# Six buffers of tap weights, due times for their steps, and sums moved from VectorE to GpSimd in a convolution with soft MoE

## The chip, the cores and the metric

The kernel runs on one core of a Trainium2 chip. Its engines are called PE (TensorE; PEld is its loading of weights), DVE (VectorE), ACT (ScalarE), POOL (GpSimd) and SP (SyncE, which issues the DMAs here). The metric is the device time of one execution in microseconds (us).

## The reference

Tokens: B = 8 sequences of S = 3584 with D = 192 channels, in 8 heads of 24. All numbers are float32. Each token brings 7 weights a head, which go through a softmax and then weigh the last 7 tokens; the result x goes through a soft MoE of 8 experts with 4 slots each.

```
w = weight_gen - max(weight_gen, -1);  w = exp(w);  w = w / (sum(w, -1) + 1e-9)
x[b,s,h,:] = sum over k of w[b,s,h,k] * x_pad[b, s+k, h, :]      # 6 zeros in front
logits = x @ phi                                                 # 28672 x 32
d = exp(logits - logits.max(0));  d /= d.sum(0) + 1e-9           # over the tokens
slot_in = d.T @ x;  per expert: slot_out = relu(slot_in @ w1[e]) @ w2[e]
c = exp(logits - logits.max(1));  c /= c.sum(1) + 1e-9           # over the slots
out = c @ slot_out
```

## The kernel before

**Convolution.** A group is 104 tokens of one sequence, 4 blocks of 26. On PE a block and head quartet is one matmul of a 128x26 band against 100 columns of x: the band holds the 7 weights of each token on its diagonals, so that 32 rows of x (for each of 4 heads) give 26 tokens. Seven groups are a *step* s (40 steps), two groups are a *pair* (140 pairs), eight pairs are a *unit* (16 units of 8 pairs and two of 6). So a step is 3.5 pairs. The sum of a token's weights comes out of the same matmul, from a column of ones in x, and the division is done behind it.

**The chain of taps of one step.** The raw weights ("taps") of a step are loaded by SP (`loadw`, 196 KB, L178); DVE takes the maximum of each seven (`tap_top`, L185); POOL subtracts it in place (`tap_sub`, L190); ACT takes the exponential and puts it into `places` (`tap_exp`, L199, two instructions); DVE transposes 32 x 32 blocks into `byrow` (`tap_turn`, L203); and POOL multiplies that by a mask into the band, in two halves of two instructions each (`band_make`, L214, columns 0 to 14 and 14 to 28; an operation of 588 elements a partition and one of 140). There are NTAP = 4 buffers of taps, two of the maxima, NPL = 2 of `places` and `byrow`, NBAND = 3 bands. x is loaded in half steps by four DMAs each (`loadx`, L175) into NXH = 5 buffers.

**The rest of the loop.** Behind `conv` (L238) of a pair: ACT copies the sums of weights (`ws`, L248), DVE takes their reciprocal (L254) and multiplies (L259, into `tm`), PE transposes (L273, `pt`), ACT copies that out (L278, `cm`). Once per unit PE makes the logits (L302), DVE the columns' maximum (L309, L311 `mq`), PE turns it (L325), ACT the exponential, DVE a transpose (L347, `dt`), and PE the dispatch (L366, `acb`). The logits are saved in `LT`, in 16 halves of sequences of 18 or 17 groups.

**Order.** The order of DVE, ACT, POOL and PE is the order in which the program emits their instructions; SP's queue is in order, and its DMAs are issued one after the other, each after the waits of its own buffer. The opening (L377 to L431) is written by hand. The loop comes from a planner: `op(engine, cost, reads, writes, f, ...)` adds an operation with an estimated cost, `late` is time that its result needs beyond the engine's, and `due` is how long behind its readiness it is to begin at the latest. `model` (L622) computes from these the latest start of each and lays them out engine by engine, the one with the earliest latest start first; its order of starts is the order of emission (L688). The times in it are estimates of the planner.

**Behind the loop** the experts are computed, and then comes the *stores' part*: for each of 49 pieces of the output PE multiplies c with the slots' outputs (`rows`, L821), DVE or ACT evicts the result from PSUM into `big` (`leave`, L828), and SP stores it (L830). c is made from `LT` by `soft`, in seven steps per half: row maximum (DVE, L78), subtraction (POOL, L80), exponential (ACT, L83), row sum (DVE, L86), + 1e-9 (ACT, L88), reciprocal (DVE, L90), multiplication (POOL, L92). Five halves are done in the loop, some behind it, and eight in the stores' part, one step per part; `turn` (L450, DVE) transposes a finished half for PE.

Of the kernel before, what the change touches and what calls it, by code (L numbers as in the profile page):

```python
# [10 lines left out]
ALU = mybir.AluOpType  # L11
# [30 lines left out]
def conv_soft_moe(ctx, tc, xh, wh, phi, w1a, w1b, w2, out):  # L42
# [30 lines left out]
    def soft(pool, h, step):  # L73
# [10 lines left out]
        elif step == 3:  # L84
            sm = sms[h] = pool.tile([128, 18, 1], F32, tag="sm", name=f"sm{h}", bufs=4)[:, 0:n]
            V.tensor_reduce(out=sm, in_=lt, axis=AX.X, op=ALU.add)  # L86
# [17 lines left out]
    NTM, NCV, NTAP, NPL, NBAND = 2, 4, 4, 2, 3  # L104
# [36 lines left out]
    for t in places:  # L141
        G.memset(t, 0.0)
# [5 lines left out]
    make_identity(nc, ident)  # L148
    near = keep.tile([128, 128], F32, name="near")
# [227 lines left out]
    loadw(0)  # L377
    loadx(0)
    loadw(1)
# [10 lines left out]
    A.copy(xbd[:, 2:4, 1], zero.unsqueeze(1).to_broadcast([128, 2, HBC * GX]))  # L390
    warm(1)
    band_make(0, 0, 8, V)
    tap_top(1)
    G.memset(xbd[:, 2:4, 0], 0.0)
    tap_sub(1, G)
    G.memset(xbd[:, 2:4, 2], 0.0)
    tap_exp(1)
    for h in (0, 1):
        G.memset(xbd[:, 4, h], 0.0)
# [13 lines left out]
    for h in (2, 3):  # L413
        A.copy(xbd[:, 4, h], zero.to_broadcast([128, HBC * GX]))
    band_make(0, 22, HB, V)
    loadx(4)
    for t in tms:
        V.memset(t[:, :, 0:1], 1.0)
        V.memset(t[:, :, 2 * D + 1 : 2 * D + 2], 1.0)
    band_make(1, 6, 14)  # L420
    conv_inv(0)
    conv_out(0)
    conv_out(1)
    band_make(1, 14, HB)
# [5 lines left out]
    for q in range(4):  # L430
        G.memset(qneg[32 * q : 32 * q + 32, q : q + 1], -1.0)  # L431

# [78 lines left out]
    for late, what in ((1.0, x_of(2)), (1.7, x_of(3)), (0.0, ("w", 2)), (1.0, ("w", 3)),  # L511
                       (5.0, x_of(4)), (0.0, ("band", 1, 0)), (2.5, ("band", 1, 1)),
                       (2.5, ("r", 1))):
# [5 lines left out]
    for k in range(1, SLOTS):  # L519
# [32 lines left out]
        for s in made.get(k, ()):  # L552
            op(VE, 0.5, [("w", s % NTAP)], [("top", s % 2)], tap_top, s)
            op(PO, 0.85, [("top", s % 2)], [("w", s % NTAP)], tap_sub, s)
            op(AC, 0.75, [("w", s % NTAP)], [("pl", s % NPL)], tap_exp, s)
            op(VE, 0.6, [("pl", s % NPL)], [("r", s % NPL)], tap_turn, s)
# [382 lines left out]
```

## Time and profile before

| | |
|---|---|
| median of 3 runs | 331.64 us (330.34 to 334.37) |
| the profiled execution | 332.66 us |
| its span in the profile | 330.9 us |
| mean granted TensorE clock | 0.935 |
| busy: PE, PEld, DVE, ACT, POOL | 275.4, 209.1, 248.3, 165.4, 202.6 us |
| DMA | 72.77 MB, mean 220 GB/s |
| first store issued | 268.91 us |

The times in the profile are those of one execution, counted from the span's start. A row of the timeline has start, length, engine, line, operation, output <- input, shape and count, and in brackets the engine's idle time before it with what ended it. A row of the windows has its length, the busy time of PE, PEld, DVE, ACT and POOL with the numbers of instructions, the granted clock (1.00 is full), the DMA share and GB/s.

### The profile page before, as it was taken

The numbers are of one execution on the slowest core, as the hardware profiler recorded it, in microseconds if no ns is written. First come the engines' busy times: TensorE is split into PE (matmuls) and PEld (weight loads), VectorE is DVE, ScalarE is ACT, GpSimd is POOL, SyncE is SP. The second block draws the span as 40 slices with busy tenths as digits, with TensorE's granted clock in tenths as the row PEclk, the third lists the DMA queues.
The fourth block names the chain that finished last, engine by engine and source line by source line (L and its number), as shares of the span: only waits on it lengthen the run. The fifth ranks groups of instructions, "written<-read, shape, count | busy, mean of one in ns | idle before, by whom it ended". The sixth has DMA issues, their size and how long they took to land.

```text
span 330.9 us, 16312 instructions
## 1 busy us (share of the span) xinstructions
PE 275.4 (83%) x6816; PEld 209.1 (63%) x6816; DVE 248.3 (75%) x549; ACT 165.4 (50%) x469; POOL 202.6 (61%) x265
## 2 busy tenths in 40 slices
PE   7779799999999988999799969899978976777500
PEld 6657678787788776888688858788857821212100
DVE  6676688888898987888687688787646689999500
ACT  7466254565645654555365445554441356656300
POOL 8989366977879786787767648487005554740000
PEclk9799799999999999999999999999999995579855
DMA  4565657676766657766776576666892049999995
GB/s 136 152 195 163 183 154 231 187 204 184 218 189 205 187 145 216 205 187 173 210 210 204 166 203 182 202 188 172 306 414 113 4 155 371 365 387 398 402 401 230
DMA packets 33000, 72.77 MB, mean 220 GB/s; under 512 B 7072, under 2 KB 12576, under 8 KB 32928
## 3 DMA queue, kind: packets, MB, share of 16 engines
q1 hardware_dynamic: 32928, 71.74, 67.9%
q8 instruction: 54, 0.88, 1.1%
q14 instruction: 18, 0.15, 0.2%
HBM read 49.35 MB, written 22.36 MB: 217 GB/s over the span
## 4 chain that ended last, share of the span: by engine, by line
PE 55%; DMA 14%; DVE 10%; POOL 7%; issue 5%; ACT 3%; SPq 1%; DVEq 0%; ACTq 0%; POOLq 0%
PE cv L238 25%; PE pt L273 12%; PE acb L366 6%; DMA out<-big 6%; PE ls L302 6%; POOL band L214 4%; DMA big<-xh 4%; DMA taps<-wh 4%; DVE big L828 2%; PE hpb L752 2%; PE so L773 2%; PE po L821 1%; POOL taps L190 1%; DVE sm L86 1%; SPq L175 1%
## 5 line engine op out<-in xcount | busy, mean ns | idle before, releaser
L214 POOL TENSOR_TENSOR band<-byrow,mask 128x588 f32<-128x588 f32 (+3 forms) x158 | 120.7, 795 | 41.9 <-DVE byrow L203 37.8
L238 PE MATMUL cv<-big,band 128*26 128x100 f32 x4480 | 121.2, 253 | 12.8 <-DVE band L214 3.6
L238 PEld LDWEIGHTS cv<-big,band 128*26 128x26 f32 x4480 | 103.1, 128 | 26.1 <-issue 16.7
L259 DVE TENSOR_TENSOR tm<-cv,ws 128x384 f32<-128x384 f32 x140 | 71.8, 551 | 6.2 <-DVE ws L254 0.9
L278 ACT COPY cm<-pt 128x312 f32<-128x312 f32 x140 | 52.1, 424 | 46.8 <-PE pt L273 46.1
L248 ACT ACTIVATE ws<-cv,eps 128x16 f32<-128x16 f32 x140 | 38.1, 273 | 55.9 <-PE cv L238 45.7
L273 PE MATMUL pt<-ident,tm 122*128 122x122 f32 x420 | 59.7, 278 | 1.8 <-ACT cm L278 1.8
L273 PEld LDWEIGHTS pt<-ident,tm 122*128 122x128 f32 x420 | 43.6, 142 | 18.1 <-issue 9.6
L821 PE MATMUL po<-cT,so 32*128 32x468 f32 (+3 forms) x256 | 32.2, 713 | 12.0 <-DVE big L828 11.3
L190 POOL TENSOR_TENSOR taps<-taps,top 128x392 f32<-128x392 f32 x39 | 34.0, 877 | 10.1 <-DVE top L185 5.5
L254 DVE RECIPROCAL ws<-ws 128x32 f32<-128x32 f32 x70 | 23.7, 339 | 20.9 <-ACT ws L248 20.4
L821 PEld LDWEIGHTS po<-cT,so 32*128 32x128 f32 (+1 forms) x256 | 8.8, 185 | 34.9 <-DVE big L828 30.5
L828 ACT COPY big<-po 128x936 f32<-128x936 f32 (+2 forms) x25 | 22.4, 898 | 16.8 <-PE po L821 9.6
L302 PE MATMUL ls<-cm,phi_sb 128*32 128x208 f32 (+1 forms) x576 | 29.2, 334 | 1.4 <-issue 1.3
L185 DVE TENSOR_REDUCE top<-taps 128x56 f32<-128x392 f32 x40 | 21.7, 548 | 11.1 <-DMA taps<-wh 8.1
L366 PE MATMUL acb<-tm,dt 128*32 128x193 f32 x536 | 27.9, 340 | 2.0 <-DVE dt L347 1.5
L828 DVE COPY big<-po 128x884 f32<-128x884 f32 (+2 forms) x24 | 25.4, 1067 | 3.2 <-DMA out<-big 3.0
L199 ACT ACTIVATE places<-taps 128x196 f32<-128x196 f32 x80 | 25.5, 378 | 3.9 <-POOL taps L190 3.7
L203 DVE STREAM_TRANSPOSE byrow<-places 128x448 f32<-128x448 f32 x40 | 25.2, 631 | 2.6 <-ACT places L199 1.5
L92 POOL TENSOR_TENSOR LT<-LT,sm 128x576 f32<-128x576 f32 (+1 forms) x16 | 18.1, 1131 | 12.1 <-DVE sm L90 12.0
L80 POOL TENSOR_TENSOR LT<-LT,rm 128x576 f32<-128x576 f32 (+1 forms) x16 | 18.0, 1131 | 10.7 <-DVE rm L78 10.7
L302 PEld LDWEIGHTS ls<-cm,phi_sb 128*32 128x32 f32 x576 | 18.9, 109 | 6.2 <-issue 2.0
(109 smaller groups left out, 224.4 us busy)
## 6 DMA issues: line engine op xcount, KB each, us to landing
big<-xh SPq DMA_DIRECT2D x320, 87.5 KB, 3.2
out<-big SPq DMA_DIRECT2D x23, 468.0 KB, 6.1
out<-big SPq DMA_DIRECT2D x24, 442.0 KB, 5.8
taps<-wh SPq DMA_DIRECT2D x40, 196.0 KB, 3.3
big<-w SPq DMA_DIRECT2D x8, 768.0 KB, 7.6
w1a_sb<-w1a SPq DMA_DIRECT2D x16, 256.0 KB, 3.1
w1b_sb<-w1b SPq DMA_DIRECT2D x8, 256.0 KB, 3.7
out<-big SPq DMA_DIRECT2D x2, 234.0 KB, 2.4
```

What stands on the lines that cost most here:

```text
L190: eng.tensor_tensor(out=r, in0=r, in1=tops.pop(s).to_broadcast([128, 2 * TJ, KT]), op=ALU.subtract)
L199: A.activation(to, taps[s % NTAP][:, b].rearrange("p (a q) k -> p a q k", q=KT), AF.Exp)
L214: eng.tensor_tensor(out=w[:, j : j + n, l].rearrange("p (a k) l -> p a k l", k=k), in0=r[:, 0:k].unsqueeze(1).to_broadcast([128, n // k, k ...
L238: P.matmul(cv[32 * blk : 32 * blk + T, o : o + 4 * GX], bands[s % NBAND][:, :, bc], xbd[:, j % NXH, :, b * GX : (b + 1) * GX], start=True, ...
L248: A.activation(wss[p // 2][:, p % 2], cvs[p % NCV][:, 0 : 16 * GX].rearrange("p (h w) -> p h w", w=GX)[:, :, GW:], AF.Identity, bias=eps[: ...
L259: V.tensor_tensor(out=tms[u % NTM][:, pr, 1 : 2 * D + 1].rearrange("p (h w) -> p h w", w=GW), in0=cv[:, :, 0:GW], in1=wss[p // 2][:, p % 2 ...
L273: P.transpose(pt[:, i, 0:TR], tm[0:TR, pr, 1 + 128 * i : 129 + 128 * i], ident[0:TR, 0:TR])
L278: copy(cms[u][:, pr].rearrange("p i b j -> p (i b) j"), pts.pop(p).rearrange("p i (b j) -> p (i b) j", j=32)[:, :, 0:T])
L302: P.matmul(lp[32 * blk : 32 * blk + 32, 0:n, par, 0:T], phi_sb[:, 2 * par + i, :], cm[:, 0:n, 1 if i else 2 * par, blk, :], start=(i == 0) ...
L366: P.matmul(ac[32 * q : 32 * q + 32], dt[:, g, :], tm[:, g // 2, o : o + D + 1], start=(g < 4), stop=(g + 4 >= 2 * n))
L821: P.matmul(po[dst : dst + hi - lo, at, 0 : n * T], so[32 * q : 32 * q + 32, lo:hi], cT[32 * q : 32 * q + 32, g0 : g0 + n, 0:T], start=True ...
L828: (V.tensor_copy if done[1] % 2 else A.copy)(ot.rearrange("p (q c) -> p q c", c=n * T), po[:, 0 : len(qs), 0 : n * T])
```

## The change

- NTAP is 6 instead of 4: taps of step s + 5 are loaded where those of s + 3 were.
- In the planner maximum, subtraction, exponential and turn of a step get due times (14, 3, 3 and 4), the bands a lower cost (1.6 instead of 1.8) with `late` 0.5, other costs are adjusted to three digits, and steps up to 2 are left out of it, since the opening has them now.
- The opening is written in another order: taps of step 1 ahead of x, taps of steps 4 and 5 behind `loadx(4)`; maximum, subtraction and exponential of step 1 ahead of the bands of step 0; those of step 2 are in the opening, its subtraction and the second half of the bands of step 1 on DVE; the zeroing of `xbd` (= `big`) is spread in another way over POOL and ACT, and the zeroing of `places` stands behind that of `ident`.
- In the stores' part the row sum is a tree on GpSimd: five additions of 16, 8, 4, 2 and 1 columns of each group's 32, instead of one reduction on DVE. In the loop and behind it the sums stay on DVE.
- Of the first 30 evictions DVE takes two of five instead of every second one (24 of all 49 before, 21 now), ACT the others.

```diff
+    def total(pool, h, to, lt, eng):
+        if eng is V:
+            V.tensor_reduce(out=to, in_=lt, axis=AX.X, op=ALU.add)
+            return
+        n, w = lt.shape[1], NS // 2
+        t = pool.tile([128, 18, w], F32, tag="tree", name=f"tree{h}")[:, 0:n]
+        G.tensor_tensor(out=t, in0=lt[:, :, 0:w], in1=lt[:, :, w:], op=ALU.add)
+        while w > 1:
+            w //= 2
+            G.tensor_tensor(out=t[:, :, 0:w] if w > 1 else to, in0=t[:, :, 0:w],
+                            in1=t[:, :, w : 2 * w], op=ALU.add)
...
-            V.tensor_reduce(out=sm, in_=lt, axis=AX.X, op=ALU.add)
+            total(pool, h, sm, lt, eng)
...
-    NTM, NCV, NTAP, NPL, NBAND = 2, 4, 4, 2, 3
+    NTM, NCV, NTAP, NPL, NBAND = 2, 4, 6, 2, 3
...
     loadw(0)
+    loadw(1)
     loadx(0)
-    loadw(1)
     loadx(1)
     loadw(2)
...
+    tap_top(1)
     tap_turn(0)
-    G.memset(xbd[:, 2:4, 3], 0.0)
+    tap_sub(1, G)
+    tap_exp(1)
     A.copy(xbd[:, 2:4, 1], zero.unsqueeze(1).to_broadcast([128, 2, HBC * GX]))
+    A.copy(xbd[:, 2:4, 3], zero.unsqueeze(1).to_broadcast([128, 2, HBC * GX]))
...
     band_make(0, 0, 8, V)
-    tap_top(1)
...
-    tap_sub(1, G)
...
-    tap_exp(1)
...
     tap_turn(1)
-    loadw(3)
     loadx(2)
     loadx(3)
+    loadw(3)
...
-    band_make(0, 16, 22, V)
+    band_make(0, 16, 24, V)
     band_make(1, 0, 6)
...
+    band_make(0, 24, HB, V)
...
+    band_make(1, 6, 14)
...
+    loadx(4)
+    loadw(4)
+    loadw(5)
...
+    conv_inv(0)
+    conv_out(0)
+    conv_out(1)
+    tap_top(2)
+    tap_sub(2, V)
+    tap_exp(2)
+    band_make(1, 14, HB, V)
...
+            if s > 2:
+                op(VE, 0.53, [("w", s % NTAP)], [("top", s % 2)], tap_top, s, due=14.0)
+                op(PO, 0.88, [("top", s % 2)], [("w", s % NTAP)], tap_sub, s, due=3.0)
+                op(AC, 0.68, [("w", s % NTAP)], [("pl", s % NPL)], tap_exp, s, due=3.0)
+            op(VE, 0.63, [("pl", s % NPL)], [("r", s % NPL)], tap_turn, s, due=4.0)
...
-                op(PO, 1.8, [("r", s % NPL)], [band_of(s, h)], band_make, s, lo, hi)
+                op(PO, 1.6, [("r", s % NPL)], [band_of(s, h)], band_make, s, lo, hi, late=0.5)
...
-        (V.tensor_copy if done[1] % 2 else A.copy)(
+        (V.tensor_copy if done[1] % (5 if done[1] < 30 else 2) in (1, 3) else A.copy)(
...
-                soft(pc, i, part - first)
+                soft(pc, i, part - first, G)
```

In the opening SP's queue stands in another order. Its rows, first of before (taps_84 to taps_87 are the four buffers of taps, big holds x, a row with x4 or x8 is one or two half steps):

```order
L178 DMA taps_84<-wh 128x392
L175 DMA big<-xh 32x700 x4
L178 DMA taps_85<-wh 128x392
L175 DMA big<-xh 32x700 x4
L178 DMA taps_86<-wh 128x392
L178 DMA taps_87<-wh 128x392
L175 DMA big<-xh 32x700 x8
L406 DMA phi_sb<-phi 128x128
L175 DMA big<-xh 32x700 x4
L178 DMA taps_84<-wh 128x392
L175 DMA big<-xh 32x700 x8
```

and then now, with the buffers taps_84 to taps_89:

```order
L190 DMA taps_84<-wh 128x392
L190 DMA taps_85<-wh 128x392
L187 DMA big<-xh 32x700 x8
L190 DMA taps_86<-wh 128x392
L187 DMA big<-xh 32x700 x8
L190 DMA taps_87<-wh 128x392
L416 DMA phi_sb<-phi 128x128
L187 DMA big<-xh 32x700 x4
L190 DMA taps_88<-wh 128x392
L190 DMA taps_89<-wh 128x392
L190 DMA taps_84<-wh 128x392
L187 DMA big<-xh 32x700 x8
```

The taps of step 1 moved ahead of x, those of step 3 behind two half steps of x, and ahead of the sixth half step of x (the last row) there now stand the loads of steps 4, 5 and 6, where there was that of step 4 alone.

In the loop POOL's subtractions stand elsewhere. Before, at the bands of steps 5 and 6 (band_94 is step 5, band_92 step 6; the subtractions of steps 6, 7 and 8 are those of taps_86, taps_87 and taps_84):

```order
L214 TENSOR_TENSOR band_94<-byrow_91,mask_134 128x21x28
L214 TENSOR_TENSOR band_94<-byrow_91,mask_134 128x5x28
L190 TENSOR_TENSOR taps_86<-taps_86,top_558 128x392
L190 TENSOR_TENSOR taps_87<-taps_87,top_657 128x392
L190 TENSOR_TENSOR taps_84<-taps_84,top_792 128x392
L214 TENSOR_TENSOR band_92<-byrow_90,mask_134 128x21x28
L214 TENSOR_TENSOR band_92<-byrow_90,mask_134 128x5x28
```

Now, at the bands of steps 5 and 6 (band_96 and band_94; the subtractions of steps 7 and 8 are those of taps_85 and taps_86):

```order
L202 TENSOR_TENSOR taps_85<-taps_85,top_664 128x392
L226 TENSOR_TENSOR band_96<-byrow_93,mask_136 128x21x28
L226 TENSOR_TENSOR band_96<-byrow_93,mask_136 128x5x28
L226 TENSOR_TENSOR band_94<-byrow_92,mask_136 128x21x28
L226 TENSOR_TENSOR band_94<-byrow_92,mask_136 128x5x28
L202 TENSOR_TENSOR taps_86<-taps_86,top_796 128x392
```

Three subtractions in a row became single ones between halves of bands, each further ahead of its own band.

In the stores' part POOL's queue has the trees. Before, from the subtraction (L80) of one half to multiplications (L92) of others:

```order
L80 TENSOR_TENSOR LT<-LT,rm_5591 128x544
L80 TENSOR_TENSOR LT<-LT,rm_5629 128x576
L92 TENSOR_TENSOR LT<-LT,sm_5604 128x576
L92 TENSOR_TENSOR LT<-LT,sm_5606 128x544
L80 TENSOR_TENSOR LT<-LT,rm_5648 128x544
L92 TENSOR_TENSOR LT<-LT,sm_5626 128x576
L80 TENSOR_TENSOR LT<-LT,rm_5670 128x576
```

Now (L79 and L82 are the tree, L92 is the subtraction and L104 the multiplication):

```order
L92 TENSOR_TENSOR LT<-LT,rm_5593 128x544
L79 TENSOR_TENSOR tree_5639<-LT 128x288
L82 TENSOR_TENSOR tree_5639<-tree_5639 128x18x8
L82 TENSOR_TENSOR tree_5639<-tree_5639 128x18x4
L82 TENSOR_TENSOR tree_5639<-tree_5639 128x18x2
L82 TENSOR_TENSOR sm_5638<-tree_5639 128x18
L79 TENSOR_TENSOR tree_5663<-LT 128x272
```

Between a half's subtraction and its multiplication POOL now also issues its five additions, and the additions of other halves stand there too.

More of the change, by code (lines that the diff above doesn't have):

```diff
@@ L148, in conv_soft_moe @@
     make_identity(nc, ident)
+    for t in places:
+        G.memset(t, 0.0)
     near = keep.tile([128, 128], F32, name="near")
@@ L581, in conv_soft_moe @@
                     op(e, c, lt if step == 0 else [],
-                       [("soft", h), ("rm", h % 2)], soft, pa, h, step, due=8.0 + step)
+                       [("soft", h), ("rm", h % 4)], soft, pa, h, step,
+                       due=8.0 + step)
         if k in dispatched and UNITS[dispatched[k] + 1][1] < UP:
@@ L636, in model @@
                 last[i] = min(last[i], max(begin[j] for j in ops[i][3]) + ops[i][4])
[L637 removed]
+        free = {TE: 0.0, VE: 2.5, AC: 0.3, PO: 1.8, SP: 0.0}
         ends, at = [None] * len(ops), [0.0] * len(ops)
```

38 lines of the change are left out of this document (12 added, 26 removed).

## Prediction

> **What bounds the kernel now.** I began with the waits of the whole span (engine and line, what it waited for, us in total, times, longest) and with the long middle stretch, in which nearly all of the 18 units are convolved.
>
> ```profile
> DVE top L185 <- DMA taps<-wh: 8.1, 6, 2.8
> ...
> POOL band L214 <- DVE byrow L203: 37.8, 23, 4.7
> ```
>
> ```profile
> 32.00:232.00 200.00, 187.72 (x5274) 154.58 (x5262) 161.34 (x379) 106.35 (x346) 146.35 (x184) 0.99 0.68 191
> ```
>
> DVE's maximum waits 8.1 us for taps, in six times, and POOL's bands 37.8 for the turned taps; whether that costs anything, the loop must tell. In the 200 us of the windows row (columns: length, busy time of PE, weight loads, DVE, ACT, POOL, the granted clock, the DMA share, GB/s) PE is busy for 187.72, and no other engine for more than 161.34. PE bounds the loop, and what a change can win there is PE's lost time. To see how much that is I took one PE operation that comes once per unit, the logits of L302, and read its starts in the timeline:
>
> ```profile
> 26.81 0.36 PE L302 MATMUL ls<-cm,phi_sb 128*32 128x208 f32 x4
> ...
> 175.33 0.36 PE L302 MATMUL ls<-cm,phi_sb 128*32 128x208 f32 x4
> ...
> 187.35 0.36 PE L302 MATMUL ls<-cm,phi_sb 128*32 128x208 f32 x4
> ...
> 228.13 0.36 PE L302 MATMUL ls<-cm,phi_sb 128*32 128x208 f32 x4
> ```
>
> The unit from 175.33 to 187.35 has no stall: 12.02 us for 8 pairs, so a step of 3.5 pairs takes about 5.26. From 26.81 to 228.13 there are 15 more such intervals, 201.32 us; at 12.02 they would take 180.3. **21.0 us of the loop are stalls.** The next rows say which of them belong to the chain of taps (load, maximum, subtraction, exponential, turn, band):
>
> ```profile
> 33.80 0.56 DVE L185 TENSOR_REDUCE top<-taps 128x56 f32<-128x392 f32 x1 [2.98 <-POOL band L214]
> ...
> 35.21 0.50 PE L238 MATMUL cv<-big,band 128*26 128x100 f32 x8 [1.79 <-POOL taps L190]
> ...
> 190.32 0.56 DVE L185 TENSOR_REDUCE top<-taps 128x56 f32<-128x392 f32 x1 [2.76 <-DMA taps<-wh]
> ...
> 193.42 0.25 PE L325 MATMUL acb<-mq,sel 128*32 128x5 f32 x8 [2.82 <-DVE mq L311]
> ...
> 208.37 0.56 DVE L185 TENSOR_REDUCE top<-taps 128x56 f32<-128x392 f32 x1 [2.18 <-DMA taps<-wh]
> ...
> 209.86 0.37 PE L366 MATMUL acb<-tm,dt 128*32 128x193 f32 x4 [1.05 <-DVE dt L347]
> ```
>
> ```profile
> DMA to landing us min/median/max: 4.3/4.3/4.3
> ```
>
> ```profile
> 31.95:35.36 3.41, 1.56 (x60) 1.18 (x55) 1.55 (x4) 0.80 (x3) 3.41 (x6) 1.00 0.64 166
> 35.36:38.78 3.42, 3.42 (x45) 2.43 (x41) 2.89 (x7) 0.27 (x1) 0.49 (x1) 0.50 0.67 187
> ```
>
> At 190.32 DVE stands still in front of the maximum L185 for 2.76 us, until the taps land; the small work behind it on DVE (mq, L311) is late, and PE waits 2.82 at 193.42. The same happens at 208.37, where PE loses 1.05. At 33.80 the page names a band as the releaser, but that load was issued at 29.37 and took 4.3 us (the landing row is of this one issue), so it landed at about 33.7: a third wait for taps. PE loses 1.79 at 35.21, and then half its clock: it was busy 1.56 of 3.41 us, and the next 3.42 were granted at 0.50, where about 1.6 us of work is lost. So late taps cost 2.82 + 1.05 + 1.79 + 1.6, with some tenths of slower starts around them (measured start to start), **7.9 us**.
>
> ```profile
> 81.94 0.31 PE L238 MATMUL cv<-big,band 128*26 128x100 f32 x4 [0.50 <-POOL band L214]
> ...
> 124.00 0.52 PE L238 MATMUL cv<-big,band 128*26 128x100 f32 x13 [1.02 <-POOL band L214]
> ...
> 124.13 0.37 SPq L178 DMA_DIRECT2D taps<-wh  x1
> ...
> 129.35 0.40 PE L238 MATMUL cv<-big,band 128*26 128x100 f32 x8 [1.56 <-DMA big<-xh]
> ...
> 158.74 0.32 PE L238 MATMUL cv<-big,band 128*26 128x100 f32 x4 [0.42 <-POOL band L214]
> ```
>
> Three bands came late (0.50 + 1.02 + 0.42, start to start **2.65**). At 124.13 SP had stood before a taps load until the exponential had freed its buffer; the x behind it in that queue came late, and PE lost 1.56 at 129.35 (start to start **1.8**). The remaining 8.7 of the 21.0 are stalls that this change doesn't touch, most of them the "issue" kind.
>
> **The change, part by part.** *Loop.* With six buffers a load is issued two steps earlier, 10.5 us, against a longest wait of 2.8. The 7.9 go, and I see no transfer that comes later for it: the number of bytes and the x loads' places in the queue behind the first steps stay. The due times put maximum, subtraction, exponential and turn ahead: in the new program most turns stand 2 to 6 pairs further before the pair that uses their band (step 8: 8 instead of 4; step 10: 11 instead of 5; step 31: 10.5 instead of 4.5). Each pair is 1.5 us of PE (12.02 / 8). That covers the 2.65 of late bands and, since the exponential is earlier and SP waits for it, the 1.8. Removable: 7.9 + 2.65 + 1.8 = 12.3. What is late next: steps 20 and 22 keep a lead of 4 and 3 pairs (3 and 5 before), and the maxima, now early, stand before work of other chains on DVE; a subtraction that POOL can't take, because its bands wait for free band buffers, leaves ACT in front of the exponential. No row shows these waits; from below they cost 0, from above, at the price of the worst band wait above (1.02) at four places and another half clock (1.6), 5.7, and I take 3.8, nearer to the upper end since leads of 3 pairs are those at which a band was late before. **Loop: −8.5**, between −12.3 and −6.6.
>
> *Opening.* Steps 1 and 2 of the chain go ahead of x and of bands:
>
> ```profile
> 9.88 0.35 PE L238 MATMUL cv<-big,band 128*26 128x100 f32 x5 [1.51 <-DVE band L214]
> ...
> 19.84 1.18 POOL L214 TENSOR_TENSOR band<-byrow,mask 128x588 f32<-128x588 f32 x1 [1.45 <-DVE byrow L203]
> ...
> 20.38 1.59 SPq L175 DMA_DIRECT2D big<-xh  x1
> ...
> 21.45 0.40 PE L238 MATMUL cv<-big,band 128*26 128x100 f32 x8 [1.11 <-POOL band L214]
> ...
> 23.07 0.31 PE L238 MATMUL cv<-big,band 128*26 128x100 f32 x4
> ```
>
> Before, the band of step 2 could start at 19.84, behind its turn. In the new order the chain of step 2 stands before the second band of step 1, and counted with the durations of the trace its turn is done by about 14.8; the pair that waited until 21.45 then can start near 18. The next pair (23.07) needs x that SP issued from 20.38 on; two more taps loads of 196 KB now stand before it in that queue, though its buffer is free sooner, so I put the pair at 20.3: 2.8 earlier. The wait of 1.51 at 9.88 shrinks too, but it lies before the same x. I take −3, between −1 (x as late as now) and −4. Inside it is a loss on DVE, which now takes the subtraction of step 2 and half a band beside POOL's work:
>
> ```profile
> 8.52 1.46 DVE L214 TENSOR_TENSOR band<-byrow,mask 128x252 f32<-128x252 f32 x4
> ...
> 8.69 0.97 POOL L190 TENSOR_TENSOR taps<-taps,top 128x392 f32<-128x392 f32 x1 [0.36 <-DVE top L185]
> ...
> L214 DVE TENSOR_TENSOR band<-byrow,mask x10: 166/306/887, 6.6 to 11.7; 128x252 f32<-128x252 f32 x3, 128x60 f32<-128x60 f32 x3, 128x336 f32<-128x336 f32 x1, 128x80 f32<-128x80 f32 x1
> ```
>
> The longest of DVE's ten bands took 887 ns where the median is 306; it is one of the four that start at 8.52, and POOL subtracted beside it from 8.69 on. So 0.6 us more per meeting, and with two or three meetings about 1.5 us, not all of it before PE. The Trainium skill ("SBUF — State Buffer", section "Who interferes with whom") says that a DVE instruction with two SBUF inputs and a GpSimd one that reads SBUF exclude one another for the whole instruction; the 887 agrees, and taken strictly, with each meeting as long as POOL's 0.87 and 1.18 us, the opening would give −2.5 instead of −3.
>
> *Stores' part.* Here DVE is full and the DMAs are nearly so:
>
> ```profile
> 268.00:304.00 36.00, 25.14 (x196) 6.54 (x190) 35.91 (x54) 23.59 (x36) 17.71 (x16) 0.76 0.92 361
> ...
> 272.00:304.00 32.00, 21.66 (x169) 5.41 (x160) 31.91 (x48) 20.20 (x32) 14.45 (x13) 0.73 0.97 379
> ...
> 300.00:320.00 20.00, 9.13 (x88) 2.40 (x84) 10.56 (x11) 7.56 (x9) 0.00 (x0) 0.80 1.02 401
> ```
>
> ```profile
> L86 DVE TENSOR_REDUCE sm<-LT 128x18 f32<-128x576 f32 x4 | 2.8, 707 | 0.0
> ...
> L828 DVE COPY big<-po 128x936 f32<-128x936 f32 x11 | 12.3, 1117 | 0.6 <-DMA out<-big 0.5
> L828 ACT COPY big<-po 128x936 f32<-128x936 f32 x12 | 11.2, 934 | 4.3 <-DMA out<-big 1.9 <-PE po L821 1.7 <-ACT sm L88 0.5
> ```
>
> ```profile
> L214 POOL TENSOR_TENSOR band<-byrow,mask 128x588 f32<-128x588 f32 x77 | 91.0, 1182 | 41.9 <-DVE byrow L203 37.8 <-PE pt L273 2.4 <-PE cv L238 1.6
> L214 POOL TENSOR_TENSOR band<-byrow,mask 128x140 f32<-128x140 f32 x77 | 32.6, 423 | 0.0
> L92 POOL TENSOR_TENSOR LT<-LT,sm 128x576 f32<-128x576 f32 x8 | 9.3, 1157 | 6.6 <-DVE sm L90 6.5
> ```
>
> ```profile
> 302.33 0.72 DVE L450 STREAM_TRANSPOSE cT<-LT 128x544 f32<-128x544 f32 x1
> ```
>
> ```profile
> out<-big SPq DMA_DIRECT2D x23, 468.0 KB, 6.1
> ```
>
> Undisturbed stores move 401 GB/s, those from 272 to 304 379: 32 × (1 − 379/401) = 1.8 us is all that a freer DVE can win. DVE loses eight sums (8 × 0.7) and three evictions (3 × 1.1), 8.9 of 36 us; ACT gains 3 × 0.93. POOL gains eight trees. From 588 elements at 1182 ns and 140 at 423, one POOL operation costs 186 ns + 1.69 ns per element; the tree of 18 rows writes 288, 144, 72, 36 and 18: 5 × 0.186 + 558 × 0.00169 = 1.9 us, in place of 0.707 on DVE. POOL then has 17.7 + 15 = 32.8 of 36 us. That fits, with 1.5 us to spare before the last turn (302.33). No row shows POOL on pieces of 8, 4 and 2 elements; from below a tree costs one 576-element operation (1.16), from above five of them (5.8). I take the line, which three sizes of row lie on: **−1.2**.
>
> The sum: −3 − 8.5 − 1.2 = −12.7 against the profiled execution's own 332.66 (its span 330.9 and 1.8 around it), so 320.0. That execution lies 1.0 above the median of the runs, so I predict **319** beside 331.64.
>
> **Rivals.** (a) *The new order only moves the stalls.* Every due time is a planner's estimate, and POOL's bands are paced by three buffers whatever stands ahead. For it: the leads of steps 20 and 22. Against: three waits of the loop are a DMA's, which no order restores. Then the loop gives about half, −4.5, and the opening −1.5: 332.66 − 7.2 − 1.0, about 325. (b) *The taps are not the bound.* SP still waits for each exponential at the same place of its queue, and an earlier load could take the DMA share (0.68) that x needs; then x is late where the taps were. Loop −2.65, opening −2, stores 0: 327. (c) *Slower: GpSimd's trees bound the stores.* Pieces of a few elements may cost POOL far more than the line. The last turn starts at 302.3; A store of 468 KB lands 6.1 us after its issue and takes 1.17 at 401 GB/s, so five are queued. POOL has until the last turn, plus two of these five (2.3 us): 302.3 − 268 + 2.3 − 17.7 = 18.9 us for eight trees. From 2.36 us a tree on, 8T − 18.9 is added, and above 3.8 us the kernel is slower than before; at the upper end (5.8) it is +27.5, so 332.66 − 11.5 + 27.5 − 1.0, about 348. The Trainium skill ("GPSIMD Engine Reference", section 4.1 "Engine selection") speaks for this side: it puts free-axis reductions on VectorE and calls two-input elementwise work on GpSimd about twice as slow. By it the tree is a loss of engine time, as in the sum above (1.9 for 0.7), and no row here shows more. (d) *Lock.* DVE and POOL in each other's way take all of the opening's gain: 322.
>
> **How the numbers follow.** Forecast 0.53 (313 to 324), (a) 0.22, (b) 0.10, (c) 0.06, (d) 0.09. The low end is the sum with all bounds good: 332.66 − 1.0 − 12.3 − 4 − 1.8 = 313.6; the high end takes in (a), (b) and (d): 313 to 328. A change below 2%, 6.6 us, is about what a measurement of this kernel can't tell from none: faster means below 325.0, which holds nearly all of the forecast and of (d) and a third of (a): 0.69. (c), in its milder half, and the rest give 0.26 and 0.05.
>
> **What would show it.** Right: no DVE wait for taps over 0.5 us behind the opening; intervals of L302 near 12.3 on average instead of 13.4; the granted clock at 1.0 in the slices at 32 to 40 us; the first L302 near 24; DVE below 30 of the first 36 us of the stores, with 390 GB/s or more. Wrong: PE waits for x where it waited for bands; trees above 2.4 us each; waits of ACT for POOL's subtraction; or the logits' interval unchanged although DVE's waits for the taps are gone. The biggest risk in the sum is the 3.8 for new stalls, which no row measures.

## The result, and the profile after

The changed kernel takes 334.53 us (median) where the kernel before takes 330.68: a ratio of 1.0122 (95% interval 1.0088 to 1.0157), 4 us slower, where 319 was forecast and at most 328 allowed. The opening got faster, by less than forecast; that the loop did isn't shown; the stores' part lost more than was won. Some executions of any of these kernels are a per cent or two longer than the rest: ratios leave them out, medians don't. Stage by stage, from the profiled executions:

| | before | after | forecast |
|---|---|---|---|
| first logits (end of the opening) | 26.81 | 25.88 | −3 |
| 15 intervals of logits (loop) | 201.3 | 198.8 | −8.5 |
| first store issued | 268.91 | 266.69 | |
| first store issued to last store landed | 61.0 | 65.6 | −1.2 |

The loop's 2.5 us lie within what profiles of one loop differ by: the loop of before took 196.6 to 201.3 in its own profile and in those of four runs below that change only the stores (198.8 on the mean), the changed loop 198.8 to 199.7 in three (199.1). The first logits do part: 26.4 to 27.3 in these five profiles, 25.7 to 26.2 in these three.

The timeline's two rows of the logits after, and the windows of the loop and of the first 36 us of the stores (columns as before):

```profile
25.88 0.36 PE L314 MATMUL ls<-cm,phi_sb 128*32 128x208 f32 x4
...
224.67 0.36 PE L314 MATMUL ls<-cm,phi_sb 128*32 128x208 f32 x4
```

```profile
32.00:232.00 200.00, 189.92 (x5309) 156.45 (x5313) 162.52 (x384) 106.69 (x346) 144.52 (x181) 0.99 0.65 192
...
268.00:304.00 36.00, 25.48 (x152) 8.48 (x148) 23.44 (x36) 21.19 (x34) 31.38 (x54) 0.67 0.84 330
```

In the stores DVE is free now (23.44 of 36 us busy instead of 35.91), but the DMAs move 330 GB/s instead of 361: 36 × (361 − 330)/401 = 2.8 us lost there, although the first store of before comes only 0.9 us into this window. The waits of the whole span show that the taps' own waits went as forecast; below them stands PE's wait for x before:

```profile
POOL band L226 <- PE cv L250: 17.9, 13, 3.9
POOL band L226 <- DVE byrow L215: 17.3, 9, 3.9
...
PE cv L250 <- DMA big<-xh: 7.2, 7, 2.2
...
DVE top L197 <- DMA taps<-wh: 2.2, 3, 1.0
```

```profile
PE cv L238 <- DMA big<-xh: 2.1, 3, 1.6
```

DVE waits 2.2 us for taps instead of 8.1, POOL 17.3 for turned taps instead of 37.8. In their place POOL's bands wait 17.9 us for PE to free a band buffer (1.6 before), as rival (a) had said of the three buffers, and PE waits 7.2 us for x (2.1 before).

### The profile page after: what moved, and what is told of

Its sections match the earlier page's. It is cut to its first block, busy times and chain, and to the rows that moved or that the text cites. A ratio compares the mean times of both kernels' runs of the same rounds, so it can differ in the third digit from the quotient of the medians.

```text
span 333.3 us, 16324 instructions
## 1 busy us (share of the span) xinstructions
PE 282.5 (85%) x6816; PEld 214.4 (64%) x6816; DVE 242.8 (73%) x541; ACT 169.3 (51%) x473; POOL 214.9 (64%) x301
## 5 line engine op out<-in xcount | busy, mean ns | idle before, releaser
L226 POOL TENSOR_TENSOR band<-byrow,mask 128x588 f32<-128x588 f32 (+3 forms) x156 | 119.7, 796 | 37.9 <-PE cv L250 17.9
L250 PE MATMUL cv<-big,band 128*26 128x100 f32 x4480 | 122.5, 254 | 15.1 <-DMA big<-xh 7.2
L285 PE MATMUL pt<-ident,tm 122*128 122x122 f32 x420 | 60.5, 281 | 0.7 <-ACT cm L290 0.7
L840 PE MATMUL po<-cT,so 32*128 32x442 f32 (+3 forms) x256 | 37.6, 707 | 11.4 <-ACT big L847 9.9
L202 POOL TENSOR_TENSOR taps<-taps,top 128x392 f32<-128x392 f32 x38 | 33.2, 875 | 13.4 <-ACT ws L260 5.9
L840 PEld LDWEIGHTS po<-cT,so 32*128 32x128 f32 (+1 forms) x256 | 12.5, 189 | 36.0 <-ACT big L847 23.6
L847 ACT COPY big<-po 128x936 f32<-128x936 f32 (+2 forms) x28 | 24.5, 901 | 10.2 <-PE po L840 4.7
L378 PE MATMUL acb<-tm,dt 128*32 128x193 f32 x536 | 26.6, 331 | 0.7 <-DVE dt L359 0.6
L847 DVE COPY big<-po 128x884 f32<-128x884 f32 (+2 forms) x21 | 22.3, 1066 | 5.7 <-PE po L840 3.9
L378 PEld LDWEIGHTS acb<-tm,dt 128*32 128x32 f32 x536 | 17.9, 110 | 4.2 <-DVE dt L359 1.3
L92 POOL TENSOR_TENSOR LT<-LT,rm 128x576 f32<-128x576 f32 (+1 forms) x16 | 18.0, 1132 | 3.7 <-DVE rm L90 3.7
```

The costliest lines, as they stand in the source:

```text
L202: eng.tensor_tensor(out=r, in0=r, in1=tops.pop(s).to_broadcast([128, 2 * TJ, KT]), op=ALU.subtract)
L226: eng.tensor_tensor(out=w[:, j : j + n, l].rearrange("p (a k) l -> p a k l", k=k), in0=r[:, 0:k].unsqueeze(1).to_broadcast([128, n // k, k ...
L250: P.matmul(cv[32 * blk : 32 * blk + T, o : o + 4 * GX], bands[s % NBAND][:, :, bc], xbd[:, j % NXH, :, b * GX : (b + 1) * GX], start=True, ...
L285: P.transpose(pt[:, i, 0:TR], tm[0:TR, pr, 1 + 128 * i : 129 + 128 * i], ident[0:TR, 0:TR])
L378: P.matmul(ac[32 * q : 32 * q + 32], dt[:, g, :], tm[:, g // 2, o : o + D + 1], start=(g < 4), stop=(g + 4 >= 2 * n))
L840: P.matmul(po[dst : dst + hi - lo, at, 0 : n * T], so[32 * q : 32 * q + 32, lo:hi], cT[32 * q : 32 * q + 32, g0 : g0 + n, 0:T], start=True ...
```

## Experiments: the stores' part

Each run is compared with runs of the kernel before on the same chip. Ratios come with 95% intervals; "stores" is first store issued to last landed and "loop" the 15 intervals of logits, both from the run's one profile.

**The parts of the change alone.** The change with the stores' part of before:

```diff
-        (V.tensor_copy if done[1] % (5 if done[1] < 30 else 2) in (1, 3) else A.copy)(
+        (V.tensor_copy if done[1] % 2 else A.copy)(
...
-                soft(pc, i, part - first, G)
+                soft(pc, i, part - first)
```

> The changed kernel with the stores' part of before (sums on DVE, every second eviction on DVE): opening and loop of the change alone. In the two traces the first store comes 2.2 us earlier and the stores take 4.5 us longer. Theory S (the trees cost the 4.5, and opening and loop are a small gain): about 328.5 where before has 330.7, first store near 266.7, from the first store to the end as before, 61 to 61.5 us. Rival R (the stores start 2 us earlier at another place of the throttle's or the DMAs' rhythm and are slow for that): stores' part over 64 us, time as the changed kernel, 334.

Ratio 0.9962 (0.9919 to 1.0005), stores 61.0, loop 199.7, first store at 266.40. The stores are back to their time though they start as early as in the changed kernel: theory S, not R. From 268 to 304 us their DMAs move 381 GB/s, so against stores that start at the same time the trees lose 36 × (381 − 330)/401 = 4.6 us, the whole loss.

The kernel before with `total()` of the change and `soft(..., G)` in the stores, nothing else:

> The kernel before with only the eight sums as trees on GpSimd, evictions as before. Theory S1 (POOL in its order is the stores' bound, and ACT and DVE stand behind its results with the evictions): the stores' part 4 to 5 us longer, 335. Rival S2 (it is the eviction split, more evictions queued on ACT behind ACT's small steps, that costs): no more than +1, 331.7. A gain of 1 would be my forecast's term.

336.05 us, ratio 1.0139 (1.0069 to 1.0209), stores 64.8. The trees alone cost as much as the whole change.

The kernel before with only the new split of evictions (the first two lines of the diff above, reversed):

> The kernel before with only the new split of evictions (DVE 21 of 49 instead of 24). Theory S1: DVE is full in that part, so relief by 3 evictions is worth 0.5 to 1.5, 329.5. Rival S2: ACT's evictions wait behind its small steps, +2 to +4, 333 to 334.5.

Ratio 0.9967 (0.9917 to 1.0016): not clear of nothing. In this run's profile and in those of six later ones with old sums and new split the stores took 60.3 to 60.6 instead of 61.0, so S1's sign, at its low end. S2 falls.

**Why a tree costs.** The rows of one tree after (by shape, mean ns):

```profile
L79 POOL TENSOR_TENSOR tree<-LT 128x288 f32<-128x288 f32 x4 | 3.2, 800 | 0.0
...
L82 POOL TENSOR_TENSOR tree<-tree 128x144 f32<-128x144 f32 x4 | 1.9, 487 | 0.3
...
L82 POOL TENSOR_TENSOR tree<-tree 128x72 f32<-128x72 f32 x4 | 1.3, 333 | 0.3
...
L82 POOL TENSOR_TENSOR tree<-tree 128x36 f32<-128x36 f32 x4 | 1.0, 245 | 0.3
...
L82 POOL TENSOR_TENSOR sm<-tree 128x18 f32<-128x18 f32 x4 | 0.9, 218 | 0.3
```

Together 2.08 us, and with the gaps between dependent additions 2.35 from the start of one tree to that of the next (269.33 to 271.68). So the price was near the line I had drawn (1.9), and at the very threshold (2.36) below which rival (c) charged nothing. The loss has another mechanism, which the timeline shows around 290 us:

```profile
289.28 0.92 ACT L847 COPY big<-po 128x936 f32<-128x936 f32 x1
...
290.25 1.86 PE L840 MATMUL po<-cT,so 32*128 32x442 f32 x8 [2.79 <-ACT big L847]
290.51 1.19 POOL L82 TENSOR_TENSOR tree<-tree 128x136 f32<-128x136 f32 x3
291.79 0.22 POOL L82 TENSOR_TENSOR sm<-tree 128x17 f32<-128x17 f32 x1
...
292.04 0.31 ACT L100 ACTIVATE sm<-sm,eps 128x17 f32<-128x17 f32 x1 [1.83 <-POOL sm L82]
292.25 1.76 ACT L847 COPY big<-po 128x936 f32<-128x936 f32 x2
292.38 0.27 DVE L102 RECIPROCAL sm<-sm 128x17 f32<-128x17 f32 x1 [4.19 <-ACT sm L100]
292.56 1.02 DVE L847 COPY big<-po 128x884 f32<-128x884 f32 x1
```

ACT's small step L100 stands in ACT's queue ahead of two evictions and waits 1.83 us for a tree; DVE's reciprocal L102 stands ahead of DVE's eviction and waits 4.19 for ACT. From 286.1 to 292.2 only ACT's 0.92 us at 289.28 are an eviction, PE had waited 2.79 us for PSUM to come free before 290.25, and from 288 to 292 the DMAs move 162 GB/s. Over the window from 268 to 304 the rows of ACT and DVE leave 13.2 us in which neither evicts, where it was 8.2 before. To tell this order (theory O) from POOL's mere lack of time (theory T), I spread the steps of six halves so that subtraction and tree lie one part further ahead of their readers, with the trees as they are:

```diff
-    making = {h + 3: 0, h + 4: 0, h + 5: 1, h + 6: 2, h + 7: 4, h + 8: 5, h + 9: 6, h + 10: 8}
+    making = {h + 3: 0, h + 4: 0, h + 5: 0, h + 6: 1, h + 7: 3, h + 8: 4, h + 9: 5, h + 10: 7}
...
-            if 0 <= part - first < 7:
-                soft(pc, i, part - first)
+            gaps = (0, 1, 2, 3, 4, 5, 6) if i < h + 5 else (0, 1, 3, 4, 6, 7, 8)
+            if part - first in gaps:
+                soft(pc, i, gaps.index(part - first), G)
```

> The kernel before with the eight trees on GpSimd, but for six of the eight halves the subtraction and the sum are each two parts ahead of the step that uses them (nine parts a half instead of seven, started one part sooner). POOL's work is the same as with the trees alone (336.05). Theory O (the order costs: ACT's and DVE's evictions stand behind their small steps, which wait for POOL): the stores' part returns to 61 to 62 us, 331 to 332. Theory T (POOL has no time left: 17.7 us of its own and eight trees of 2.35 us start to start are 36.5 us from 265.7, whatever the order): 64 us or more, 334 to 336.

Ratio 1.0003 (0.9952 to 1.0053), against 1.0139 for the same trees unspread; stores 61.8 instead of 64.8. (Over all its twelve executions the median is 333.97, against 331.41 for before: up to 2.6 us of the time stay open, and the stores' 61.8 is one profile, against two with unspread trees, 64.8 and 65.6.) The windows of the trees alone, and of the trees spread:

```profile
268.00:304.00 36.00, 31.28 (x148) 9.02 (x148) 25.79 (x39) 18.40 (x31) 32.10 (x55) 0.57 0.85 333
```

```profile
268.00:304.00 36.00, 27.47 (x164) 8.74 (x160) 27.24 (x40) 20.20 (x32) 32.08 (x55) 0.62 0.93 366
```

POOL does the same work in the same time (32.10 and 32.08 of 36 us, 55 instructions), and the DMAs get 366 GB/s instead of 333. The time in which neither engine evicts falls from 13.3 to 10.1 us. Theory O holds and T falls; T keeps at most the 0.8 us that are left to 61.0. Which wait went is told by the waits from 265 to 306 us, of the trees alone and of the trees spread:

```profile
ACT sm L100 <- POOL sm L82: 11.2, 7, 2.2
...
DVE sm L102 <- ACT sm L100: 7.0, 5, 3.2
```

```profile
ACT sm L100 <- POOL sm L82: 9.7, 7, 2.3
...
DVE sm L102 <- ACT sm L100: 0.9, 1, 0.9
```

ACT still stands before the trees; it is DVE, with its evictions, that no longer stands behind ACT. PE's granted clock differs too: 0.76 before, 0.67 after, 0.57 with the trees alone and 0.62 with them spread. It doesn't order the runs, since the spread trees move 366 GB/s at 0.62 and the changed kernel 330 at 0.67; what it adds was not separated.

The kernel before with only the first addition on POOL, and DVE's reduction over the 16 columns left:

```diff
+        G.tensor_tensor(out=t, in0=lt[:, :, 0:w], in1=lt[:, :, w:], op=ALU.add)
+        V.tensor_reduce(out=to, in_=t, axis=AX.X, op=ALU.add)
...
-            V.tensor_reduce(out=sm, in_=lt, axis=AX.X, op=ALU.add)
+            total(pool, h, sm, lt, eng)
```

> The kernel before with only the first addition of each tree on GpSimd (0.80 us), and DVE's reduction over the 16 columns that are left (half as long, about 0.4 us instead of 0.7). Both theories O and T expect a relief, of different size. T: POOL's work falls to 17.7 + 6.9 us, the stores' part is 60 to 61 us, 330 to 331, and DVE's relief of 2.4 us may show as -0.5. O: one wait more in the chain of a half (POOL, then DVE, then ACT) with evictions behind each, still 1 to 2 us lost: 332 to 333.

Ratio 0.9987 (0.9948 to 1.0026), stores 60.8: no loss, and no gain to speak of for 2.1 us less on DVE.

## Experiments: the loop

**Whose wait it was.** The forecast counted 2.65 us at 81.94, 124.00 and 158.74 as late bands, since the profile names POOL's band there. Rows of the kernel before that I had not asked for: the last two of the four x loads that these same matmuls need, in the timeline of SP's queue, and the landing times of each of these three pairs, in the same order:

```profile
78.01 0.88 SPq L175 DMA_DIRECT2D big<-xh  x2
...
118.87 0.88 SPq L175 DMA_DIRECT2D big<-xh  x2
...
154.22 0.88 SPq L175 DMA_DIRECT2D big<-xh  x2
```

```profile
DMA to landing us min/median/max: 3.3/3.4/3.5
...
DMA to landing us min/median/max: 4.4/4.5/4.6
...
DMA to landing us min/median/max: 3.9/4.1/4.2
```

The second of each two issues starts about 0.46 after the first, so x landed at 81.8, 123.75 and 158.6, within 0.25 us of the matmuls at 81.94, 124.00 and 158.74; at 35.21, which I had put to late taps, x had landed at 35.01. Bands and x were late together. Taking away the bands' and the taps' part could gain a few tenths there, not 2.65 + 1.79 and the half clock behind it.

**Buffers.** Six buffers of taps alone:

```diff
-    NTM, NCV, NTAP, NPL, NBAND = 2, 4, 4, 2, 3
+    NTM, NCV, NTAP, NPL, NBAND = 2, 4, 6, 2, 3
...
     loadx(4)
+    loadw(4)
+    loadw(5)
```

> The kernel before with only six buffers of taps (taps of steps 4 and 5 loaded behind the fifth half step of x; costs, due times, opening and stores as before). Theory Q (x, not the taps, is what comes last at most stalls of the loop: at 35.2, 81.9, 124.0, 129.4 and 158.7 of before x landed within 0.3 us of the matmul): only the waits at 193 and 210 go, -2 to -4.5, 326.5 to 328.5, with more waits for x early on since two more loads stand ahead of x. Rival P (my forecast's: the taps' loads are the bound): -6 to -8, 323 to 325.

330.81 us, ratio 1.0013 (0.9961 to 1.0064): nothing, below even theory Q. DVE waits only 0.3 us for taps in its profile; x and bands took their place. The loop took 194.7 there, less than in any profile of the loop of before, but from the 16th logits to the first store it was 44.6 us instead of 40.8.

Six buffers of x, and six of both:

```diff
-    w1a_sb = keep.tile([128, E, F], F32, name="w1a_sb")
+    w1a_sb = keep.tile([128, E // 2, F], F32, name="w1a_sb")
-    NXH, HBC = 5, NBC // 2
+    NXH, HBC = 6, NBC // 2
```

> The kernel before with six x buffers instead of five (four buffers of taps as before). To make room the first weights of experts 4 to 7 are loaded into the space of those of experts 0 to 3, and the hidden layer of these four uses them: that part of the computation is changed, the number of loads and of instructions is not. Theory Q (the x loads, late in SP's queue, are what comes last at most stalls of the loop): each x load may be issued 2.6 us sooner, the loop's 15 intervals of logits take 190 to 194 us instead of 197 to 201, the time 323 to 326; waits for taps stay. Theory P (taps): nothing or up to -2, since the taps are as late as before. Theory N (neither: the loop's stalls come from elsewhere, and x is only just in time because SP has no reason to be earlier): nothing.

> The kernel before with six x buffers and six buffers of taps (the same space for the experts' first weights, the same part of the computation changed). Theory Q: the taps' relief now shows, since x no longer hides it: 2 to 4 us below the kernel with six x buffers alone, 320 to 323. Theory P: as six buffers of taps alone did, 330. Theory N: 330.

335.94 and 336.44 us, ratios 1.0121 and 1.0135. In these two the loads of the experts' second weights also go to other places of `big` than the free ones; their last units took 22.4 and 27.2 us instead of 18.6, so I read only the 15 intervals: 198.2 and 197.6. With six of x PE's wait for x is nearly gone, and PE waits for DVE instead, which itself stands 12.0 us before taps in the whole span. PE's waits from 26 to 232 us:

```profile
PE acb L366 <- DVE dt L347: 5.5, 4, 2.7
PE acb L325 <- DVE mq L311: 3.5, 3, 2.5
...
PE cv L238 <- DMA big<-xh: 0.2, 1, 0.2
```

With six of both x was late again at four places, 4.0 us. Theory N's numbers, then; but most waits had changed their names.

**SP's queue.** SP's queue has hardly a gap: of 32 to 232 us the rows of its 335 issues take 175.5, and the other 24 lie between them, 0.05 us each in the median, so an issue comes every 0.6 us. Part of the rows is waiting: 46 are longer than 0.5 us, and in 15 of these a buffer came free only inside the row, 14.5 us in all. One run with x in pairs of half steps, one of the changed kernel with that and the old sums, and two with the experts' first weights (`w1`) in half and in double the number of DMAs:

```diff
+        for h in range(4):
+            SY.dma_start(xbd[32 * h : 32 * h + 32, j % NXH : j % NXH + 2, h],
+                         xh[j // 2, h].rearrange("r (p c) -> r p c", p=2))
...
-                            op(SP, 0.4, [], [], SY.dma_start, to[:, e, f], w[:, e, f])
+                            op(SP, 0.4, [], [], SY.dma_start, to[:, e], w[:, e])
...
-                            e, f = j // 2, slice(F // 2 * (j % 2), F // 2 * (j % 2 + 1))
+                            for i in (2 * (j % 2), 2 * (j % 2) + 1):
+                                e, f = j // 2, slice(F // 4 * i, F // 4 * (i + 1))
```

> The kernel before, but in the loop the two half steps of x of one step are loaded by four DMAs instead of eight wherever their buffers stand side by side (four of five steps); bytes, rows and buffers are the same, the taps as before. Theory I (SP's issuing is the loop's pace: from 32 to 232 us it issued 335 DMAs, busy for 175.5 us and 0.05 us between any two, so 0.59 us each, 5.7 us for the 9.65 of a step, against 5.26 that PE needs): SP has 3.2 DMAs a step less, 3.8 us a step, and x stops being late; the taps' waits stay: loop 188 to 193 instead of 197 to 201, time 322 to 326. Theory B (bytes in flight and not their number set the pace, the long issues are the DMAs' own back-pressure): no change, 330 to 332, or slower since a load now waits for two buffers.

> The changed kernel with the stores' sums back on DVE (the new split of evictions stays) and x loaded in pairs of half steps. Theory I: with SP out of the way the six buffers and the due times show what they are worth, 3 to 6 us below the kernel before with pairs: 317 to 321. Theory B: as the changed kernel with the stores of before, 330.

> The kernel before with the first weights of the experts loaded in 12 DMAs of 512 KB instead of 24 of 256 KB, spread over the same steps. Theory I: 12 DMAs less, 7 us of SP, of which the loop gets 2 to 5: 327 to 329. Theory B: none, or +1 as x stands behind longer transfers, 331 to 332.

> The kernel before with the first weights of the experts in 48 DMAs of 128 KB instead of 24 of 256 KB. Theory I: 24 DMAs more on SP, 14 us; since SP and PE are nearly level now, most of it is added: +7 to +14, 338 to 345. Theory B: the same bytes, +0 to +2, 331 to 333.

Measured: 1.0021 (0.9978 to 1.0063), 0.9990 (0.9939 to 1.0041), 1.0162 (1.0115 to 1.0209) and 1.0342 (1.0286 to 1.0399); loops 196.8, 194.7, 200.2 and 207.1. More issues cost what theory I says (24 × 0.6 = 14 us of SP; 3.4%, some 11 us). Fewer bring nothing in the time, although the loop of the changed kernel gets 4 us shorter with pairs: its first logits come at 29.7 instead of 26.2 (28.0 instead of 26.8 in the kernel before), so what the loop won the start had lost, and theory I is not refuted by these two. 12 long ones cost 5 us, 4 of them in the last two units (22.7 us instead of 18.6 in the profile), which neither theory had. PE's waits from 26 to 232 us, for x pairs, for `w1` in 512 KB and for `w1` in 128 KB:

```profile
PE cv L247 <- issue: 2.6, 5, 1.6
PE acb L375 <- issue: 1.8, 3, 1.1
...
PE cv L247 <- DMA big<-xh: 1.1, 2, 0.8
```

```profile
PE cv L238 <- issue: 6.3, 6, 2.5
PE cv L238 <- DMA big<-xh: 1.4, 1, 1.4
```

```profile
PE cv L238 <- DMA big<-xh: 10.1, 10, 2.2
```

With `w1` in short DMAs x is late and the "issue" waits are gone; in long ones it is the other way round. What "issue" is here can be read from the DMA records, in which the profile keeps the program's own instructions apart (rows of the kernel before: packets, MB, share of the 16 DMA engines):

```profile
q1 hardware_dynamic: 32928, 71.74, 67.9%
q8 instruction: 54, 0.88, 1.1%
```

The 54 packets have 16 KB each. Seven profiles (before, after, the new evictions, six buffers of taps, both with x in pairs, and `w1` in 512 KB) have 31 "issue" waits of PE over 0.4 us between 30 and 240 us; all 31 end 1.2 to 1.7 us after such a packet was moved, while packets come some 4.7 us apart. Since 13,632 of the 16,312 instructions are PE's, PE most likely waits for its own code there, whose packets go through the same 16 engines as x, taps and `w1`. What makes the code late is not shown.

**Less to move.** Only 4 of the 24 loads of `w1`, in the loop of before and in that of the change (old sums, new split):

```diff
-                        if 1 + 3 * j // 2 == s:
+                        if 1 + 3 * j // 2 == s and j // 2 in (0, E):
```

> The kernel before, loading only 4 of the 24 pieces of the experts' first weights (expert 0's, used for all experts; the other 20 loads, 5 MB, are left out). Theory D (the transfers together, by SP's issues and by what stands in their queues, set the loop's pace): x and fetch waits fall, the loop takes 189 to 194 us instead of 195 to 201, the time 323 to 327. Theory C (the chain of taps sets it): the taps' waits at the same steps stay, and the loop gains under 2.

> The changed kernel with sums on DVE in the stores' part (new evictions), with the same 20 loads left out. Theory D: now six buffers and due times are worth something, since the transfers have room: 3 to 6 us below the kernel before with the same loads left out, 318 to 322. Theory C: as far below it as the changed loop is with all loads, 0 to 2 us.

324.13 and 319.19 us: 0.9787 (0.9725 to 0.9848) and 0.9613 (0.9545 to 0.9681). These kernels leave out 20 loads and use the weights that are loaded for all experts. Theory D in both times: the loop of before goes to 189.6 with x waits of 0.3 us, and now the change's opening, buffers and due times are worth 4.9 us (324.1 to 319.2), of which the stores' new split is some 0.5. Where they are won is not shown: in the one profile of the changed kernel, an execution of 322.39 us, the loop took 192.6, longer than 189.6, and the gain lay between the 16th logits and the first store (45.1 us and 40.2).

**What is left of the change, and a way around the two ends.** The change without its trees; that with x in pairs and `w1` in 128 KB; and that with `w1` issued by ACT in 24 and in 48 pieces:

```diff
-                            op(SP, 0.4, [], [], SY.dma_start, to[:, e, f], w[:, e, f])
+                            op(AC, 0.4, [band_of(s, 1)], [], A.dma_start, to[:, e, f], w[:, e, f])
```

> The changed kernel with the stores' sums on DVE and the new split of evictions: everything of the change but the trees. The parts alone gave -0.4% (opening, loop, buffers) and -0.3% (evictions): together -0.5 to -0.9%, 328.5 to 330, the stores' part 60 to 60.5 us. If the change's trees are not the whole of the loss, 331 or more.

> The changed kernel with sums on DVE, x loaded in pairs of half steps (3.2 DMAs a step less) and the experts' first weights in 48 pieces of 128 KB (0.6 a step more). With pieces of 128 KB PE's waits for nothing the profile shows fell from 6 to 9 us to 3.5, and SP's late x cost 12.8; with pairs x cost nothing and those waits 11.6. Theory D with its two ends (SP's number of issues makes x late, long transfers make PE's instruction fetches late): both small, loop 188 to 192, 323 to 326. If the fetch waits come from the pairs of x themselves, loop 194 to 196, 330.

> The changed kernel with sums on DVE, the 24 loads of the experts' first weights issued by ACT, each behind the bands of its step, instead of SP. If SP's issuing is what they cost: x is no longer late, the loop 190 to 194, time 321 to 325 (without the loads it was 319.2, with them on SP 328.9). If their bytes cost: 327 to 329 as before. If ACT is held up by issuing (0.42 us each, in order, ahead of its copies): 330 or more, with DVE and PE behind ACT.

> The same with 48 pieces of 128 KB on ACT. If long transfers make PE's instruction fetches late, 1 to 3 us below the run with 24 pieces; if ACT is held up by issuing, 3 to 10 above it.

Measured: 0.9890 (0.9805 to 0.9975), 0.9894 (0.9829 to 0.9958), 1.0007 (0.9953 to 1.0062) and 0.9954 (0.9909 to 1.0000). The first two beat the kernel before by 1.1% by the ratio; their medians are 328.92 and 327.68, against 331.48. Pairs and short pieces so add nothing to what the sums on DVE give, where 323 to 326 was expected; the loop is 5 us shorter (193.9 instead of 198.9), but the first logits come at 29.9 instead of 26.2. From ACT's queue the same bytes bring nothing:

```profile
PE cv L250 <- issue: 5.0, 6, 1.6
...
PE acb L378 <- DVE dt L359: 1.1, 3, 0.5
```

(PE's waits of the 24 pieces from 26 to 232 us.) x is never late there, and PE has the "issue" waits instead. So it is not SP's issuing alone that `w1` costs. Nor does the length of its DMAs decide the "issue" waits: with pieces of 128 KB they are gone where x is late (10.1 us, above), and add up to 6.9 and 6.8 us (those over 0.4, from 30 to 240 us) with x in pairs and on ACT's queue. Whether it is the bytes as such, or how many loads stand in the queues at once, these runs don't tell.

## Why the prediction was wrong, step by step

- **Stores, −1.2, measured +4.5.** The failed step is "That fits, with 1.5 us to spare before the last turn": POOL's time did fit, and the tree's price was only 0.2 to 0.45 us off, but I added up POOL's work and never asked who stands behind the one that waits for it. DVE's reductions had been in the queue of the engine that evicts; on POOL their result came back over ACT's L100 and DVE's L102, each ahead of evictions. Rival (c) had the right place and side, and the wrong mechanism: by its 8T − 18.9 the measured tree costs nothing, while spreading the same trees takes most of the stores' loss away (64.8 to 61.8, where 61.0 is without trees). The 1.8 us that the relief of DVE could win was a fair bound: old sums with the new split gained about 0.5 of it.
- **Loop, −8.5, measured −2.5 in the two profiles, and about nothing over all eight.** Four steps. "Three bands came late" and the third wait for taps: x landed within 0.25 us of the same matmuls, so 2.65 and 1.79 of the 12.3 were hardly there. "At 124.13 SP had stood before a taps load" (1.8): that load began 0.1 us behind the issue before it; the long row there is an x issue of 2.37 us from 120.26. "I see no transfer that comes later for it": from 26 us on PE waits 4.5 us for x instead of 2.1; that a PE that stalls less asks for x sooner would explain it, but isn't shown. And the 3.8 us for new stalls was too little: with 20 loads fewer both kernels gain, so the transfers have a part in the loop's pace. Rival (b), 327 by x in place of taps, named this at 0.10, and the change without trees gives 328.9. The taps' waits themselves (193 and 210) did go. "Most of them the 'issue' kind", of the 8.7 left over, doesn't hold either: PE's waits of that kind add up to 2.2 us from 26 to 232.
- **One execution.** The profile of before had a long loop: the same loop took 196.9, 199.0, 200.3 and 196.6 in the profiles of the four runs that changed only the stores, with stalls of other sizes and places. Of the 21.0 us that I took apart, up to 4.7 belonged to that execution.
- **Opening, −3, measured −0.9.** The chain of taps went as worked out:

```profile
12.72 0.31 PE L250 MATMUL cv<-big,band 128*26 128x100 f32 x4 [2.14 <-DMA big<-xh]
...
14.37 1.56 POOL L226 TENSOR_TENSOR band<-byrow,mask 128x588 f32<-128x588 f32 x2 [0.81 <-DVE byrow L215]
...
22.51 0.31 PE L250 MATMUL cv<-big,band 128*26 128x100 f32 x4 [0.61 <-DMA big<-xh]
```

  The band of step 2 starts at 14.37 instead of 19.84, and PE then stands before x at 12.72 and 22.51. The failed term is x at 20.3: it landed at 22.4, 0.4 sooner than before, behind the taps loads that were put ahead of it. The row at 20.38 that I had read is the half step behind the one that this pair needs; that one was issued from 17.64 on and landed at 22.8.
- **Lock.** I charged 1.5 us. One meeting is seen, a 40-element operation of DVE at 622 ns; the large ones ran beside POOL's memsets (588 elements in 765 ns, the subtraction in 568). Smaller than charged, and not on the path: the meeting is over at 9.9, and PE waits for x until 12.72.
- **The Trainium skill** ("GPSIMD Engine Reference", section 4.1 "Engine selection") puts free-axis reductions on VectorE. The runs agree with its choice: with the sums back on DVE the same kernel goes from 1.0122 to 0.9890. The price of the sum was 2.08 us for 0.707; what decided here was the order.

## What to carry over

Before work goes to an idle engine, follow its result back: which queues does it come back through, and what stands behind the instruction that waits; one part more of distance was worth 3 us of the stores here, with the same work. Where the profile names one releaser, look up when the other inputs of that instruction landed: what is second by 0.2 us takes the stall over. And a stall in one execution is a sample: weigh it by other profiles of the same code before adding it up.

## What the hardware showed that I had not expected

- Instructions of the program come in packets of 16 KB, 54 of them, through the same 16 DMA engines as data; all 31 "issue" waits of PE over 0.4 us in seven profiles end 1.2 to 1.7 us behind such a packet. They add up to 7.3 us with `w1` in pieces of 512 KB, and with pieces of 128 KB to none where x is late, but to 6.9 us with x in pairs.
- SP's issues came 0.6 us apart in the loop (0.42 for most rows; 46 of 335 longer, by 0.9 on the mean, 14.5 us of that waiting for buffers), and 24 more small DMAs made the kernel 3.4% slower, with the same bytes.
